# Windowed attention feeding a gated FFN on one core: FFN weights loaded as bf16 by casting DMAs from GpSimd's queue, with the loads metered

## The chip, the cores and the metric

The kernel runs on one core of a Trainium2 chip. The core has five engines, each with its own instruction stream: TensorE (PE; the profile shows its weight loads apart, as PEld), VectorE (DVE), ScalarE (ACT), GpSimd (POOL) and SyncE (SP, which only starts DMAs here). Sixteen DMA engines, shared by all queues, move data between HBM and the on-chip SBUF. Matmul results go to PSUM, eight banks of 512 fp32 columns per partition. The metric is the device time of one execution in microseconds.

## The reference

Sizes: 4 batches, 8 heads, 768 positions, head width 64; 4 sink positions and a window of 128; the FFN has 512 inputs, 2048 hidden units and 512 outputs. Inputs and output are float32.

```
scores = q @ k^T / sqrt(64)                       # per batch and head
keep   = (key < 4) | (0 <= query - key < 128)
a      = softmax(where(keep, scores, -1e9))
x      = (a @ v) with heads side by side          # 3072 tokens x 512
h      = x @ w_in                                 # 512 -> 2048
g      = h / (1 + exp(-beta * h))                 # beta: one per hidden unit
out    = g @ w_out                                # 2048 -> 512
```

## The kernel before

**Tiling.** The 3072 tokens are eight half batches of 384. A half batch has four head pairs, so there are 32 pairs in all, u = 0 to 31. Each pair runs through these steps. T: six transposes on TensorE bring q and k to head-major form, one copy takes both out of PSUM. SC: scores only for the key blocks that the window reaches. SS: scores against the sinks. ScalarE takes exp into bf16 tiles E and ES, and GpSimd masks E in place with affine selects (in even half batches VectorE multiplies the sink blocks with a mask). AV: E times v, with a column of ones that gives the softmax sum; VectorE takes the reciprocal and normalises. OT: three transposes and a copy into xT, the FFN's input in bf16.

**FFN.** An H unit is one block of 128 hidden units for one half batch: four matmuls of 384 columns, tanh on ScalarE, and one VectorE instruction that gives (tanh(beta h / 2) + 1) h, which is twice the gated value. An O quad is four matmuls of 512 columns; four quads make an output tile of 128 tokens, which one copy takes from PSUM to an output buffer `osb`, and SyncE stores. There are 128 H units and 96 O quads. The factor 1/2 that g lacks sits in w_out.

**Loads.** q, k and v come as float32 into two staging slots (`stg`), are cast to bf16 (x16, vaug) and used from there. The first half batch is loaded per head (24 DMAs of 96 KB, runs of 256 bytes per row; q and v on SyncE's queue, k on ScalarE's), the others per block of 128 tokens (nine DMAs of 256 KB per half batch, on SyncE's queue, 1024 runs of 256 bytes each). The weights are eight pieces of 1 MiB, 512 runs of 2 KB each: 0 to 3 are w_in by columns (piece j feeds H units 4j to 4j+3), 4 to 7 are w_out by rows (piece 4+j feeds the j-th quad of every O tile). Each piece lands in one of two staging buffers `wst` (L362) and two instructions of ScalarE or VectorE cast it into place (`cast_w`, L365; w_out times 0.5).

**The order.** A planner writes all instruction streams in one pass. It keeps a modelled clock per engine and for the DMA queue, and again and again takes the first step of the list OT, AV, SC, SS, T, then O or H, that its model says is ready; loads and casts are placed by `background()` before each choice. Each operation becomes a place in its engine's stream; engines run their streams strictly in order, and semaphores guard every dependency. So a modelled duration changes no work, only the order. Before the change `LOADS` puts the weight pieces 0 to 3 behind the first half batch, and 4 to 7 behind the second, all on SyncE's queue; a load is placed as soon as its buffer is free in the model.

Of the kernel before, what the change touches and what calls it, by code (L numbers as in the profile page):

```python
# [26 lines left out]
class Graph:  # L27
# [17 lines left out]
    def add(self, eng, fn, ns=0, r=(), w=(), x=(), dma=None):  # L45
# [182 lines left out]
def _program(nc, G, sb, ps, q, k, v, w_in, w_out, beta, out):  # L228
    NU = 2 * NPAIR
    NSTG, NX, NV, NT, NE, NON, NG, NTT, NOS, NWS, NKS = 2, 2, 3, 8, 3, 3, 3, 3, 3, 2, 4  # L230
    NK = NB // 2
# [9 lines left out]
    wst = sb("wst", (128, 4, 512), F32, NWS)  # L241
# [114 lines left out]
    def load_w(j):  # L356
        z = j % NWS
        if j < 4:
            src = w_in_src[:, :, j * 512:(j + 1) * 512]
        else:  # L360
            src = w_out_src[:, 4 * (j - 4):4 * (j - 3), :]
        add("sp", lambda e: e.dma_start(wst[z][:, :, :], src), 1048576 / 380, w=[("wst", z)], dma=f"dw{z}")  # L362

    def cast_w(j):
        z = j % NWS  # L365
        for h in range(2):
            src = wst[z][:, 2 * h:2 * h + 2, :]
            if j < 4:
                dst, sc = w_in16[:, 2 * h:2 * h + 2, j * 512:(j + 1) * 512], 1.0
            else:  # L370
                dst, sc = w_out16[:, 4 * (j - 4) + 2 * h:4 * (j - 4) + 2 * h + 2, :], 0.5
            eng = quickest({"act": act_ns(1024), "dve": dve_ns(1024, 1.9)})
            add(eng, copy_fn(eng, dst, src, sc), act_ns(1024) if eng == "act" else dve_ns(1024, 1.9),
                r=[("wst", z)], w=[("w16", j, h)])
# [208 lines left out]
    def HQ(T_, m):  # L583
# [5 lines left out]
        for c in range(4):  # L589
# [3 lines left out]
                r=[("w16", m // 4, c // 2), ("xT", c, T_)], x=[("B", bs[0])])  # L593
# [9 lines left out]
    def OQ(T_, t, j):  # L603
# [3 lines left out]
        for m in range(4 * j, 4 * j + 4):  # L607
# [3 lines left out]
                r=[("w16", 4 + m // 4, m // 2 % 2), ("g", T_, m)], x=[("B", bk)])  # L611
        if j == 3:
# [4 lines left out]
            add(eng, copy_fn(eng, osb[z][:, :], P[:, bk, :]), opts[eng], w=[("osb", z)], x=[("B", bk)])  # L617
# [16 lines left out]
    n_cast, n_w = [0], [0]  # L634

    def head(s):
# [25 lines left out]
        elif s == "H":  # L662
# [5 lines left out]
            t = G.at([("xT", c, T_) for c in range(4)] + [("w16", m // 4, 0), ("w16", m // 4, 1)])  # L668
            tb = banks_at(1)
            fn = lambda: HQ(T_, m)  # L670
        else:
# [3 lines left out]
            t = G.at([("g", T_, m) for m in range(4 * j, 4 * j + 4)] + [("w16", 4 + j, 0), ("w16", 4 + j, 1)])  # L675
# [11 lines left out]
    def background():  # L687
# [3 lines left out]
        while moved:  # L691
            moved = False
            i = done["load"]
            if i < len(LOADS):
                x = LOADS[i]
                at_hb = CASTS[n_cast[0]][0] if n_cast[0] < len(CASTS) else NSB
                if isinstance(x, int):
                    if x < NWS + n_w[0]:
                        load_w(x)
# [105 lines left out]
```

## Time and profile before

| | |
|---|---|
| median of 3 runs | 261.52 us (260.94 to 264.68) |
| profiled execution | 262.38 us |
| its span, first to last instruction | 260.7 us |
| granted TensorE clock, mean | 0.991 |
| TensorE busy | 228.8 us (88%) |
| ScalarE, VectorE, GpSimd busy | 166.5, 129.0, 96.7 us |
| read from HBM, written | 27.27 MB, 6.29 MB |
| first FFN matmul | 30.76 us |

In the profile's strips each character is a slice of 6.5 us, and a digit is the busy share in tenths. In its rows the bracket at the end gives the idle time before an instruction and what ended it; SPq, ACTq and POOLq are the engines' DMA issues. The bulk of the reads is over at about 120 us; the rest of the execution is FFN work on TensorE.

### The profile page before, as it was taken

How to read it: one execution, taken by the hardware profiler on the slowest of the kernel's cores; microseconds unless marked ns; L12 is line 12 of the kernel's file. 1: busy time of each engine (PE TensorE's matmuls, PEld its weight loads, DVE VectorE, ACT ScalarE, POOL GpSimd, SP SyncE). 2: the span in 40 equal slices, each digit the busy share in tenths (PEclk: the TensorE clock that was granted, in tenths of full speed). 3: DMA queues.
4: the chain of work that ended last, by engine and by line, in shares of the span. 5: the costliest groups of instructions: out<-in, count | busy, mean ns of one | idle time of the engine just before them, and what ended most of it. 6: DMA issues, size and time to landing. Idle time of an engine off the chain costs nothing.

```text
span 260.7 us, 5023 instructions
## 1 busy us (share of the span) xinstructions
PE 228.8 (88%) x1861; PEld 132.3 (51%) x1889; DVE 129.0 (49%) x285; ACT 166.5 (64%) x302; POOL 96.7 (37%) x197
## 2 busy tenths in 40 slices
PE   1307899669999999999999999999999999999995
PEld 0204456334556566655665655555555555555542
DVE  1116678553466686556666434633533453353320
ACT  2239689663898988888889874754545554565420
POOL 5205443665597897869791720000000000000000
PEclk9999999799999999999999999999999999999999
DMA  6984879799999999996101011011011111111112
GB/s 153 215 313 158 243 181 288 267 284 247 221 264 216 268 219 226 256 229 166 40 4 40 3 40 43 0 40 54 30 40 44 40 40 40 43 40 40 43 40 80
DMA packets 82856, 33.89 MB, mean 130 GB/s; under 512 B 75648, under 2 KB 75664, under 8 KB 82832
## 3 DMA queue, kind: packets, MB, share of 16 engines
q1 hardware_dynamic: 79632, 32.78, 46.3%
q10 hardware_dynamic: 3200, 0.79, 1.3%
q8 instruction: 15, 0.25, 0.4%
q14 instruction: 9, 0.07, 0.1%
HBM read 27.27 MB, written 6.29 MB: 129 GB/s over the span
## 4 chain that ended last, share of the span: by engine, by line
PE 68%; DMA 10%; ACT 9%; DVE 7%; SPq 2%; issue 2%; POOL 1%; DVEq 0%
PE P L590 30%; PE P L608 28%; DMA wst<-in_moe_w_out_dram 6%; ACT E L490 4%; DMA k_stage<-in_k_dram 3%; PE P L480 3%; DVE onorm L558 2%; SPq L353 2%; PE P L429 2%; PE P L570 2%; PE P L552 2%; DVE g L596 2%; ACT t L594 2%; DMA v_stage<-in_v_dram 1%; DVE qkT L307 1%
## 5 line engine op out<-in xcount | busy, mean ns | idle before, releaser
L596 DVE SCALAR_TENSOR_TENSOR g<-t,P 128x384 bf16<-128x384 f32 x128 | 70.5, 554 | 83.2 <-ACT t L594 68.8
L594 ACT ACTIVATE t<-P,hbeta 128x384 f32<-128x384 f32 x128 | 74.1, 583 | 50.3 <-PE P L590 47.3
L590 PE MATMUL P<-xT,w_in 128*128 128x384 bf16 x512 | 99.5, 330 | 0.0
L608 PE MATMUL P<-w_out,g 128*128 128x512 bf16 x356 | 93.2, 381 | 6.3 <-DVE w_out L308 2.3
L590 PEld LDWEIGHTS P<-xT,w_in 128*128 128x128 bf16 x512 | 49.6, 99 | 39.2 <-issue 2.0
L496 POOL TENSOR_SCALAR_AFFINE_SELECT E<-E 128x256 bf16<-128x256 bf16 (+1 forms) x112 | 52.8, 506 | 34.2 <-ACT E L490 33.8
L608 PEld LDWEIGHTS P<-w_out,g 128*128 128x128 bf16 x384 | 36.0, 98 | 39.6 <-DVE w_out L308 3.3
L490 ACT ACTIVATE E<-P 128x768 bf16<-128x768 f32 x64 | 45.0, 770 | 4.0 <-PE P L480 3.7
L552 PE MATMUL P<-vaug,E 128*128 128x65 bf16 x352 | 20.6, 201 | 1.2 <-POOL E L496 0.4
L309 ACT ACTIVATE osb<-P 128x512 f32<-128x512 f32 x22 | 13.2, 599 | 12.9 <-PE P L608 12.8
L552 PEld LDWEIGHTS P<-vaug,E 128*128 128x128 bf16 x352 | 17.8, 102 | 5.0 <-POOL E L496 1.4
L558 DVE TENSOR_TENSOR onorm<-P,rden 128x384 bf16<-128x384 f32 x32 | 17.8, 557 | 1.1
L480 PE MATMUL P<-qkT 64*128 64x128 bf16 (+1 forms) x256 | 16.8, 254 | 0.8 <-ACT E L490 0.8
L409 POOL TENSOR_SCALAR_AFFINE_SELECT vaug<-v_stage 128x512 bf16<-128x512 f32 x21 | 14.3, 681 | 3.7 <-DMA v_stage<-in_v_dram 3.7
L309 ACT ACTIVATE xT<-P 128x384 bf16<-128x384 bf16 x25 | 12.3, 505 | 5.3 <-PE P L570 5.1
L517 ACT ACTIVATE ES<-P 128x128 bf16<-128x128 f32 (+1 forms) x32 | 11.7, 398 | 6.0 <-PE P L514 5.8
L570 PE MATMUL P<-ident,onorm 128*128 128x128 bf16 x96 | 11.3, 230 | 3.8 <-DVE onorm L558 3.1
L429 PE MATMUL P<-ident,k_0 128*128 128x128 bf16 x48 | 6.0, 241 | 8.7 <-DVE k_0 L307 8.7
L480 PEld LDWEIGHTS P<-qkT 64*128 64x128 bf16 x256 | 9.1, 99 | 8.7 <-issue 3.2
L542 PE MATMUL P<-vS,ES 128*128 128x130 bf16 x64 | 13.4, 229 | 0.0
L429 PE MATMUL P<-ident,q_0 128*128 128x128 bf16 x48 | 6.0, 241 | 7.1 <-DVE q_0 L307 5.3
L570 PEld LDWEIGHTS P<-ident,onorm 128*128 128x128 bf16 x96 | 6.7, 100 | 9.7 <-DVE onorm L558 5.2
(47 smaller groups left out, 140.1 us busy)
## 6 DMA issues: line engine op xcount, KB each, us to landing
out_dram<-osb SPq DMA_DIRECT2D x24, 256.0 KB, 2.0
q_stage<-in_q_dram SPq DMA_DIRECT2D x21, 256.0 KB, 4.4
k_stage<-in_k_dram SPq DMA_DIRECT2D x21, 256.0 KB, 4.5
v_stage<-in_v_dram SPq DMA_DIRECT2D x21, 256.0 KB, 4.3
wst<-in_moe_w_in_dram SPq DMA_DIRECT2D x4, 1024.0 KB, 7.7
wst<-in_moe_w_out_dram SPq DMA_DIRECT2D x4, 1024.0 KB, 7.0
k_stage<-in_k_dram ACTq DMA_DIRECT2D x8, 96.0 KB, 2.9
q_stage<-in_q_dram SPq DMA_DIRECT2D x8, 96.0 KB, 2.8
```

The source lines that it names most:

```text
L309: return lambda e: e.activation(dst, src, AF.Copy, bias=0.0, scale=scale)
L429: add("pe", lambda e, i=i, n=n, c=c: nc.tensor.transpose(mp[:, i * HALF + c * 128:i * HALF + (c + 1) * 128], x16[n][hb % NX][:, c, 2 * hp: ...
L480: add("pe", lambda e, dst=dst, kt=kt, kc=kc, rows=rows, q0=q0, nq=nq: e.matmul(dst, kt[rows, 1, kc:kc + 128], qkT[u % NT][rows, 0, q0:q0 + ...
L490: add("act", lambda e, src=src, dst_=dst_: e.activation(dst_, src, AF.Exp, bias=0.0, scale=SCALE), act_ns(256 * n), w=[(k_, z, j) for k_ i ...
L496: add("gp", lambda e, d=d, sg=sg, at_=at_: e.affine_select(d, d, [[0, 2 * len(at_)], [sg, 128]], ALU.is_ge, 0.0, base=min(sg, 0), channel_ ...
L552: e.matmul(A[:, c0:c0 + D + 1], E[z][:, i, hh, :], vaug[vz][:, kb % NK, 2 * hp + hh, :], start=a, stop=o, skip_group_check=True), 39,
L558: add("dve", lambda e: e.tensor_tensor(onorm[on][:, :, :, :].rearrange("p m h d -> p (m h) d"), av[:, :, 0:D], rden[on][:, :].unsqueeze(2) ...
L570: add("pe", lambda e, m=m: nc.tensor.transpose(mp[:, m * 128:(m + 1) * 128], onorm[on][:, m, :, :].rearrange("p h d -> p (h d)"), ident[:, ...
L590: add("pe", lambda e, c=c: e.matmul(hp, w_in16[:, c, m * 128:(m + 1) * 128], xT[:, c, t0:t0 + HALF], start=(c == 0), stop=(c == 3)), mm_ns ...
L594: add("act", lambda e: e.activation(tt[ti][:, :], hp, AF.Tanh, bias=0.0, scale=hbeta[:, m:m + 1]), act_ns(HALF) + 93, r=["hbeta"], w=[("t" ...
L596: add("dve", lambda e: e.scalar_tensor_tensor(gt[T_ % NG][:, m, :], tt[ti][:, :], 1.0, hp, ALU.add, ALU.mult), dve_ns(HALF), r=[("t", ti)] ...
L608: add("pe", lambda e, m=m: e.matmul(P[:, bk, :], gt[T_ % NG][:, m, t * 128:(t + 1) * 128], w_out16[:, m, :], start=(m == 0), stop=(m == NM ...
```

## The change

The weights are no longer staged. `load_w` issues one DMA per piece from GpSimd's queue, with a float32 source and a bf16 destination, straight into `w_in16` or `w_out16`; the DMA rounds on its way. `cast_w` and the `wst` buffers are gone, H and O wait for the piece's DMA itself, each piece has a semaphore of its own, and the factor 1/2 moves from w_out to the copy of the output tile. The output buffers become four instead of three.

The planner's rules change with it. It costs a DMA issue 1150 ns on GpSimd and 550 on the other queues (before, 600 on SyncE and 1000 on the others). The first half batch's twelve loads are all placed at the start, before anything else. After that a load is placed only when the modelled DMA backlog is at most 3 us (`BACKLOG`), and a cast of q, k or v only when its data is due within 300 ns (`AHEAD`), where it was 500 and, in the first half batch, at once. When nothing is ready the model's clock moves on by 200 ns.

```diff
-            self.free[eng] = at + (600 if eng == "sp" else 1000)
+            self.free[eng] = at + (1150 if eng == "gp" else 550)
...
-    NSTG, NX, NV, NT, NE, NON, NG, NTT, NOS, NWS, NKS = 2, 2, 3, 8, 3, 3, 3, 3, 3, 2, 4
+    NSTG, NX, NV, NT, NE, NON, NG, NTT, NOS, NKS = 2, 2, 3, 8, 3, 3, 3, 3, 4, 4
...
     def load_w(j):
-        z = j % NWS
         if j < 4:
-            src = w_in_src[:, :, j * 512:(j + 1) * 512]
+            dst, src = w_in16[:, :, j * 512:(j + 1) * 512], w_in_src[:, :, j * 512:(j + 1) * 512]
         else:
-            src = w_out_src[:, 4 * (j - 4):4 * (j - 3), :]
-        add("sp", lambda e: e.dma_start(wst[z][:, :, :], src), 1048576 / 380, w=[("wst", z)], dma=f"dw{z}")
-
-    def cast_w(j):
...
+            dst, src = w_out16[:, 4 * (j - 4):4 * (j - 3), :], w_out_src[:, 4 * (j - 4):4 * (j - 3), :]
+        add("gp", lambda e: e.dma_start(dst, src), 1048576 / 380,
+            w=[("w16", j)], dma=f"dw{j}")
...
-            add(eng, copy_fn(eng, osb[z][:, :], P[:, bk, :]), opts[eng], w=[("osb", z)], x=[("B", bk)])
+            add(eng, copy_fn(eng, osb[z][:, :], P[:, bk, :], 0.5), opts[eng], w=[("osb", z)], x=[("B", bk)])
...
+    BACKLOG, AHEAD = 3000, 300
...
-            if i < len(LOADS):
+            if i < len(LOADS) and G.dma_free <= now + BACKLOG:
...
-                if t is not None and ok and (t <= now + 500 or hb == 0):
+                if t is not None and ok and t <= now + AHEAD:
...
+    for x in xl(0):
+        load(*x)
+        for c in range(NK):
+            mark(("in",) + x, ("stg", x[1], 0, c, x[3]))
+    done["load"] = 12
...
         if best[0] > now + 200:
...
+            G.free["pe"] = now + 200
+            continue
```

SyncE's stream behind the first half batch's loads, before: the four w_in pieces, then the second half batch (`128x8x64`), then w_out.

```order
L353 DMA v_stage<-in_v_dram 128x3x64 x2
L362 DMA wst<-in_moe_w_in_dram 128x4x512 x4
L353 DMA q_stage<-in_q_dram 128x8x64
...
L353 DMA v_stage<-in_v_dram 128x8x64
L362 DMA wst<-in_moe_w_out_dram 128x4x512 x4
L353 DMA q_stage<-in_q_dram 128x8x64
```

SyncE's stream now, from the seventh load of the second half batch on; the first output store stands between the fourth and the fifth load of the third.

```order
L352 DMA q_stage<-in_q_dram 128x8x64
L352 DMA k_stage<-in_k_dram 128x8x64
L352 DMA v_stage<-in_v_dram 128x8x64
L352 DMA q_stage<-in_q_dram 128x8x64
L352 DMA k_stage<-in_k_dram 128x8x64
L352 DMA v_stage<-in_v_dram 128x8x64
L352 DMA q_stage<-in_q_dram 128x8x64
L607 DMA out_dram<-osb 128x512
L352 DMA k_stage<-in_k_dram 128x8x64
```

No weight is left on SyncE's queue, the second half batch follows the first directly, and stores now stand among the early loads.

GpSimd's stream from the masks of the first four head pairs on (`E<-E`), before:

```order
L409 AFFINE_SELECT q_0<-q_stage 128x3x128 x3
L496 AFFINE_SELECT E<-E 128x256 x12
L409 AFFINE_SELECT q_1<-q_stage 128x512
L409 AFFINE_SELECT k_1<-k_stage 128x512
L409 AFFINE_SELECT vaug<-v_stage 128x8x64
```

and now, from the second pair's masks to the last weight piece, whose issue stands behind the masks of pair 4:

```order
L484 AFFINE_SELECT E<-E 128x256 x3
L361 DMA w_in<-in_moe_w_in_dram 128x4x512
...
L397 AFFINE_SELECT q_1<-q_stage 128x512
L397 AFFINE_SELECT k_1<-k_stage 128x512
L361 DMA w_out<-in_moe_w_out_dram 128x4x512
...
L397 AFFINE_SELECT vaug<-v_stage 128x8x64
L361 DMA w_out<-in_moe_w_out_dram 128x4x512
L484 AFFINE_SELECT E<-E 128x256
L484 AFFINE_SELECT E<-E 128x512 x2
L484 AFFINE_SELECT E<-E 128x256
L361 DMA w_out<-in_moe_w_out_dram 128x4x512
```

One w_in issue follows the masks of each of the first four pairs; three of the w_out issues stand among the casts of the second half batch's loads, and the fourth follows the next pair's masks.

TensorE's stream from the first use of the last w_out piece to the third half batch's transposes (`ident,q_0`), before:

```order
L608 MATMUL P<-w_out,g 128x512 x4
L542 MATMUL P<-vS,ES 128x130
L552 MATMUL P<-vaug,E 128x65 x4
...
L608 MATMUL P<-w_out,g 128x512 x4
L570 MATMUL P<-ident,onorm 128x128 x3
L608 MATMUL P<-w_out,g 128x512 x4
L590 MATMUL P<-xT,w_in 128x384 x4
...
L429 MATMUL P<-ident,q_0 128x128 x3
```

and now:

```order
L596 MATMUL P<-w_out,g 128x512 x4
L558 MATMUL P<-ident,onorm 128x128 x3
L530 MATMUL P<-vS,ES 128x130
L540 MATMUL P<-vaug,E 128x65 x4
...
L596 MATMUL P<-w_out,g 128x512 x12
L558 MATMUL P<-ident,onorm 128x128 x3
L596 MATMUL P<-w_out,g 128x512 x4
L578 MATMUL P<-xT,w_in 128x384 x4
L596 MATMUL P<-w_out,g 128x512 x4
L578 MATMUL P<-xT,w_in 128x384 x4
L417 MATMUL P<-ident,q_0 128x128 x3
```

Counted over the whole stream, 19 H units and 9 O quads stood ahead of those transposes before, and 18 and 11 now; more quads lie behind the wait for the last w_out piece.

More of the change, by code (lines that the diff above doesn't have):

```diff
@@ L751, in _program @@
                 break
-            pend = [G.at([("wstu", n_w[0])]) if n_w[0] < 8 else None]
-            if n_cast[0] < len(CASTS):
-                pend.append(G.at([("in",) + CASTS[n_cast[0]]]))
-            pend = [p for p in pend if p is not None and p > now]
-            assert pend, (done, n_cast, n_w)
-            G.free["pe"] = min(pend)
+            G.free["pe"] = now + 200
+            assert now < 1e6, (done, n_cast)
             continue
@@ L760, in _program @@
         if best[0] > now + 200:
[L761 to L767 removed]
+            G.free["pe"] = now + 200
+            continue
         fn()
```

43 lines of the change are left out of this document (8 added, 35 removed).

## The prediction

> **What bounds the kernel now.** I read the page first: busy time, then the strips of 40 slices (6.5 us each).
>
> ```profile
> span 260.7 us, 5023 instructions
> PE 228.8 (88%) x1861; PEld 132.3 (51%) x1889; DVE 129.0 (49%) x285; ACT 166.5 (64%) x302; POOL 96.7 (37%) x197
> PE   1307899669999999999999999999999999999995
> DMA  6984879799999999996101011011011111111112
> ```
>
> TensorE is the limit from about 60 us on; its idle time of 31.9 us (260.7 - 228.8) lies ahead of that, and there the DMA strip is at 7 to 9 while TensorE's falls to 0 and to 6. The stretches, cut at places in TensorE's program (the first FFN matmul at 31, the end of the first 16 H units at 43.1, the end of the last weight wait at 59, the third half batch's transposes at 67.09, the last matmuls at 250.2), say how much:
>
> ```profile
> core 0: us, PE busy (x) PEld busy (x) DVE busy (x) ACT busy (x) POOL busy (x), PEclk, DMA share, GB/s
> 0.00:31.00 31.00, 12.66 (x118) 7.72 (x119) 11.06 (x29) 15.06 (x29) 11.36 (x34) 1.00 0.74 213
> 31.00:43.10 12.10, 12.10 (x68) 6.89 (x67) 8.61 (x16) 9.38 (x17) 5.15 (x9) 1.00 0.91 211
> 43.10:59.00 15.90, 10.72 (x125) 6.21 (x124) 9.53 (x18) 11.51 (x18) 9.30 (x18) 0.89 0.86 289
> 59.00:67.09 8.09, 7.96 (x53) 4.15 (x55) 2.83 (x7) 3.15 (x6) 4.86 (x8) 1.00 1.04 236
> 67.09:250.20 183.11, 178.10 (x1471) 104.19 (x1494) 96.26 (x214) 126.25 (x232) 66.07 (x131) 1.00 0.37 95
> ```
>
> 18.3 us are idle before 31, 5.2 between 43.1 and 59, 0.1 up to 67.09, and 5.0 in the following 183. The chain of waits, in order of time, names what TensorE waits for early on:
>
> ```profile
> 10.29 8.03 DMA k_stage<-in_k_dram
> ...
> 30.97 8.85 PE P L590 x44
> ...
> 40.55 8.72 DMA wst<-in_moe_w_out_dram
> ...
> 50.62 7.25 DMA wst<-in_moe_w_out_dram
> ...
> 57.88 1.07 ACT w_out L309
> ```
>
> So the last head pair's k takes 8.03 us because it shares the engines with two pieces of w_in, and the last piece of w_out sets 59.0. SyncE's timeline shows why the engines aren't full all along: the four w_in issues stretch over 16.86 us, since pieces 2 and 3 wait for a staging buffer, and nothing behind them starts.
>
> ```profile
> 8.70 1.05 SPq L353 DMA_DIRECT2D v_stage<-in_v_dram  x2
> 9.79 16.86 SPq L362 DMA_DIRECT2D wst<-in_moe_w_in_dram  x4
> ```
>
> **The price of a transfer**, from three stretches: k and w_in together; the gap while SyncE waits; q, k, v alone.
>
> ```profile
> 13.00:16.60 3.60, 0.00 (x0) 0.00 (x0) 0.00 (x0) 2.10 (x7) 0.00 (x0) 1.00 1.02 348
> 20.00:26.70 6.70, 5.41 (x64) 3.39 (x64) 4.25 (x11) 6.37 (x12) 4.21 (x9) 1.00 0.47 159
> 34.00:39.60 5.60, 5.60 (x35) 3.35 (x34) 4.28 (x9) 5.26 (x10) 3.12 (x5) 1.00 1.01 229
> ```
>
> A half batch of q, k, v is 2.36 MB in runs of 256 B: 10.3 us at 229 GB/s. A weight piece is 1.05 MB in runs of 2 KB: 3.0 us at 348. The gap leaves 0.53 x 6.7 = 3.6 us of the engines unused.
>
> **What is removed.** The weight casts leave:
>
> ```profile
> L309 ACT ACTIVATE w_in<-wst 128x1024 bf16<-128x1024 f32 x4 | 4.4, 1095 | 0.7 <-DMA wst<-in_moe_w_in_dram 0.7
> L309 ACT ACTIVATE w_out<-wst 128x1024 bf16<-128x1024 f32 x2 | 2.1, 1058 | 2.0 <-DMA wst<-in_moe_w_out_dram 2.0
> L307 DVE CAST w_in<-wst 128x1024 bf16<-128x1024 f32 x4 | 3.2, 793 | 0.0
> L308 DVE TENSOR_SCALAR w_out<-wst 128x1024 bf16<-128x1024 f32 x6 | 4.7, 808 | 2.9 <-DMA wst<-in_moe_w_out_dram 2.9
> ```
>
> 6.5 us on ScalarE and 7.9 on VectorE, of which only the 1.07 us that begin at 57.88 end the chain; neither engine is the limit later (64% and 49% busy). The staging buffers go, and with them the waits in front of SyncE's loads: the second half batch's nine loads follow the first's at 9.8 instead of 26.7 us.
>
> **What is moved.** Eight weight issues go to GpSimd's queue. There each stands behind masks or load casts, and masks stand behind it; a masked E tile is what TensorE's AV matmuls wait for. No trace row shows an issue on GpSimd. The nearest are SyncE's: a weight issue without a wait took 0.37 us, a load of 1024 runs up to 1.40. I take 1.1, a middle nearer the upper row as GpSimd is the slower engine for all it does here. All eight k issues now stand first on ScalarE, 8 x 0.48 us from 0.81 on, so its table load ends near 6.1, about when TensorE's first transposes do; it is covered. The output copies take 0.5 as a factor in the same 24 instructions, and a fourth output buffer joins three whose stores land in 2.0 us while an O tile takes 4 x 0.86 us: nothing for both.
>
> ```profile
> L353 ACTq DMA_DIRECT2D k_stage<-in_k_dram x8: 420/480/507, 0.8 to 10.3; - x8
> L309 ACT ACT_TABLE_LOAD x1 | 1.3, 1283 | 3.7 <-DMA k_stage<-in_k_dram 3.7
> out_dram<-osb SPq DMA_DIRECT2D x24, 256.0 KB, 2.0
> 51.58 1.40 SPq L353 DMA_DIRECT2D k_stage<-in_k_dram  x1
> L362 SPq DMA_DIRECT2D wst<-in_moe_w_out_dram x4: 368/410/798, 39.6 to 50.6; - x4
> 12.63 0.53 ACT L309 ACTIVATE vaug<-v_stage 128x384 bf16<-128x384 f32 x1 [2.27 <-DMA v_stage<-in_v_dram]
> 22.49 4.34 POOL L496 TENSOR_SCALAR_AFFINE_SELECT E<-E 128x256 bf16<-128x256 bf16 x9 [10.90 <-ACT E L490]
> ```
>
> **The front.** The times in this part are estimates; they are to show that nothing there comes later than the transfers that the next part counts. Without w_in beside them, the first half batch's loads are served by about 11.5 (the last v's cast waited until 12.63, and its issue is as early as before). The last k no longer lands at 18.3 but with the rest. Scores of pair 0 start at about 7, its masks (0.48 each, from the x9 row) end near 10, where the first w_in piece is issued. Pairs 1 to 3 follow at the pace of ScalarE's work per pair (two exps, one small exp, two casts: some 2.9 us), so that the last pair's scores stand at 17, its masks at 20 and the first H matmul, after AV, normalisation, transposes and a copy (2.6 us), at about 22.6: 8 us earlier than 30.97. The w_in pieces are issued near 10, 14, 17 and 20 and, one after another, are in place by 28, each before its four H units start. The 16 units take 12.1 as before, to 34.9; the second half batch's k is cast by 36.
>
> **The gate.** The time of the last w_out piece follows from what the engines have carried before: 11.5, and 10.3 for the second half batch, and eight pieces. A casting transfer reads as much and writes half. No row shows one. Its price lies between 1.5 us (the write side decides) and 4.6 (it runs at the 229 GB/s of the small runs); I take 3.2, near the 3.0 row, as the 2 KB read is the same. Sum: 11.5 + 10.3 + 8 x 3.2 = 47.4. Beside it, packets of the third half batch slip in: k above got 192 KB through while two pieces went, which is a 256 B run per 2 KB run; four w_out pieces thus let 0.52 MB by, 2.3 us. With 1.3 to land (an output store lands in 2.0, of which its 256 KB are 0.8 to 1.1): **51.0**, where it was 57.88, with a cast to 59. The instruction order allows it: the last w_out issue stands behind pair 4's masks, which by the steps above end at about 43.4.
>
> From the gate to the third half batch's transposes the new order has 8 O quads, 2 H units, 2 AV and 3 output transposes. Prices from TensorE's timeline after 59 and in the chain:
>
> ```profile
> 59.00 1.04 PE L608 MATMUL P<-w_out,g 128*128 128x512 bf16 x4 [1.32 <-ACT w_out L309]
> 59.87 0.22 PE L542 MATMUL P<-vS,ES 128*128 128x130 bf16 x1
> ...
> 60.41 1.03 PE L608 MATMUL P<-w_out,g 128*128 128x512 bf16 x4
> 61.51 0.34 PE L570 MATMUL P<-ident,onorm 128*128 128x128 bf16 x3
> 61.69 1.03 PE L608 MATMUL P<-w_out,g 128*128 128x512 bf16 x3
> 62.55 0.81 PE L590 MATMUL P<-xT,w_in 128*128 128x384 bf16 x4
> 63.20 1.03 PE L608 MATMUL P<-w_out,g 128*128 128x512 bf16 x4
> ```
>
> O 0.86, AV 0.54, transposes 0.18, H 0.65: 6.9 + 1.3 + 1.1 + 0.5 = 9.8. The transposes start at 60.8, not 67.09. By then 18 H and 11 O are done instead of 19 and 9: 1.1 us more. Gain 6.3 + 1.1 = 7.4. From there TensorE does the same work; half batches 4 to 6 must arrive 6 us earlier relative to what the same engines carry (after the gate still 5.5 half batches, 57 us), and I give back 1.0 (0 to 3) for waits at their transposes. Span 260.7 - 6.4 = 254.3; around it lie 262.38 - 260.7 = 1.7, so 256.0 against the profiled run's 262.38. The median 261.52 is 0.9 below that run: **255.1 us**.
>
> **Two rules against these rows.** The quickest weight piece took 5.0 us from issue to landing, beside other loads:
>
> ```profile
> DMA to landing us min/median/max: 5.0/7.2/10.1
> ```
>  DMA: Bandwidth & Descriptors in the Trainium skill (section Anatomy of one DMA) gives a transfer issued from GpSimd 2.0 us plus its bytes at 436 GB/s, 4.4 us for a piece; by an estimate from it each piece holds the engines 2.4 us, the transfers alone end by 44.6, the last issue behind pair 4's masks (43.4 + 1.1 + 4.4 = 48.9) decides in their place, and the end comes 2.1 us earlier, near 253.0.
>
> VectorE is busy 8.61 of 12.10 us in 31 to 43.1. SBUF — State Buffer in the Trainium skill (Who interferes with whom) says that VectorE's two-port modes lock GpSimd out, and that a DMA issued there then waits for its descriptors; this speaks against the change, and no run here shows it yet. It is the second rival.
>
> **Rivals.** (1) *The casting path is slow.* At 4.6 us a piece the gate moves by 8 x 1.4 = 11.2 to 62.2; 7.4 - 11.2 - 1 gives a time 4.8 us longer, 266.3, and slower beyond. The sign turns at 7.4 / 8 = 0.9 us more per piece, 4.1. For it: the slow row exists and nothing shows casting; against: reads and packets stay those of the 348 row. Chance 0.14, half of it over 2% slower with prices past 4.6. (2) *GpSimd is held up.* If every issue costs 2.5 us (the 1.40 row, and 1.1 in which VectorE holds it up), masks and H slip by 1.4 for each of three issues ahead of the last pair's masks, 4.2, and the gate with them: gain 2.2, 259.3. For it: masks are on the chain already; against: VectorE loses the weight casts, its longest instructions with both ends in SBUF. Chance 0.15. (3) *A store blocks loads.* SyncE's new order puts the first output store between the fourth and fifth load of the third half batch; it waits for the first O tile, at gate + 1.5. Five loads follow, 1.31 MB, 5.7 us, landing and a cast of 0.6: ready at gate + 9.3 or later, against 9.8 when TensorE asks. Little cover: with 3 us late, 258.1. Chance 0.15. (4) The forecast: 0.56, its own range 252 to 258.
>
> **Chances.** This kernel's measurement tells 2%, 5.2 us, from no change: faster is below 256.3. The forecast gives it three times in four, (2) and (3) once in six: 0.47. Slower, above 266.8: 0.10, half of (1) and 0.03 for two rivals at once. Same: 0.43. The range 251.5 to 264 leaves out most of (1) and a little below.
>
> **What would show it.** Right: no k wait of 8 us early; the first H matmul near 22.6; w_out's last piece landed near 51; third transposes near 61; DMA share above 0.9 from 10 to 50. (1) shows as weight pieces over 4 us apart in time with a full DMA strip; (2) as long DMA issues on GpSimd with masks behind; (3) as transposes waiting on q or k casts while SyncE waits for a copy of the output.

## The result, and the profile after

The changed kernel takes 253.73 us (median of 4 runs, 253.14 to 254.02), the kernel before, on the same chip, 261.23 us (4 runs, 260.85 to 264.68). The ratio is 0.968, with a 95% interval of 0.960 to 0.977: faster. The profiled run took 254.02 us, with a span of 252.3 us. The page of the changed kernel, its busy times, strips and the two queues that carry loads and weights (packets, MB written, share of the 16 engines' span):

```profile
span 252.3 us, 5040 instructions
PE 229.4 (91%) x1889; PEld 132.0 (52%) x1889; DVE 121.8 (48%) x274; ACT 160.6 (64%) x298; POOL 100.3 (40%) x204
...
PE   1588955899999999999999999999999999999994
DMA  7999999969999899985011010111011011111112
...
q1 hardware_dynamic: 75408, 24.39, 39.5%
q0 software_dynamic: 4224, 4.19, 10.3%
```

The second and third slices of TensorE were 3 and 0 and are 5 and 8. The dip later, at 43 to 59 us before, now lies at 36 to 50. The stretches of the kernel after, cut at the same places of TensorE's program as those of before (first FFN matmul, end of the first 16 H units, last wait for a weight, third half batch's transposes):

```profile
core 0: us, PE busy (x) PEld busy (x) DVE busy (x) ACT busy (x) POOL busy (x), PEclk, DMA share, GB/s
0.00:20.28 20.28, 10.16 (x117) 7.41 (x118) 9.95 (x29) 11.42 (x24) 13.79 (x39) 1.00 1.00 199
20.28:32.36 12.08, 12.08 (x68) 6.67 (x65) 7.20 (x13) 9.10 (x16) 4.21 (x8) 0.86 1.15 217
32.36:50.21 17.85, 11.12 (x106) 5.99 (x105) 4.37 (x10) 9.86 (x16) 9.91 (x19) 0.81 1.11 188
50.21:60.19 9.98, 9.96 (x79) 5.42 (x80) 3.62 (x10) 2.27 (x4) 6.01 (x11) 1.00 0.73 180
```

The first FFN matmul came 10.5 us earlier (30.76 to 20.28). The last wait for a weight ends 8.8 us earlier (59.00 to 50.21), the third half batch's transposes start 6.9 us earlier (67.09 to 60.19), and from these to the end of the span the kernels take 193.6 and 192.1 us. So of the gain of 8.4 us in the span all but 1.5 us is made ahead of these transposes. Between 32.36 and 50.21 TensorE loses even more than in the like stretch before (6.7 us idle against 5.2), and the DMA share is 1.11 instead of 0.86: the transfers now come almost without gaps, and the work waits for the last of them. (A share can exceed 1, since it adds up the times of packets, which overlap: transfers alone and back to back read 0.91 to 1.12 in the first experiment.)

GpSimd's timeline gives the issues, and the chain of waits, in order of time, what ended last:

```profile
9.95 0.91 POOL L361 DMA_DIRECT2D w_in<-in_moe_w_in_dram  x1
...
18.69 0.76 POOL L361 DMA_DIRECT2D w_in<-in_moe_w_in_dram  x1
...
38.29 0.76 POOL L361 DMA_DIRECT2D w_out<-in_moe_w_out_dram  x1
...
40.95 0.76 POOL L361 DMA_DIRECT2D w_out<-in_moe_w_out_dram  x1
```

```profile
29.72 7.90 DMA v_stage<-in_v_dram
...
40.95 9.21 DMA w_out<-in_moe_w_out_dram
```

Two things are new there. A load of v (the last of the second half batch) takes 7.90 us beside two w_out pieces; its cast stands on GpSimd ahead of the third w_out issue and holds it until 38.29. And SyncE's fourth load of the third half batch is followed by the first output store, which waits from 42.3 to 51.9.

### The profile page after: what moved, and what is told of

The parts are those of the page before. It is cut to its first block, busy times and chain, and to the rows that moved or that the text cites. A ratio compares the mean times of both kernels' runs of the same rounds, so it can differ in the third digit from the quotient of the medians.

```text
span 252.3 us, 5040 instructions
## 1 busy us (share of the span) xinstructions
PE 229.4 (91%) x1889; PEld 132.0 (52%) x1889; DVE 121.8 (48%) x274; ACT 160.6 (64%) x298; POOL 100.3 (40%) x204
## 3 DMA queue, kind: packets, MB, share of 16 engines
q0 software_dynamic: 4224, 4.19, 10.3%
## 4 chain that ended last, share of the span: by engine, by line
PE 66%; SPq 11%; ACT 9%; DMA 7%; DVE 4%; issue 1%; POOL 1%; DVEq 0%
PE P L596 29%; PE P L578 26%; SPq L352 11%; ACT E L478 4%; DMA w_out<-in_moe_w_out_dram 4%; DMA v_stage<-in_v_dram 3%; PE P L540 2%; ACT t L582 2%; PE P L417 2%; PE P L558 2%; PE P L468 2%; DVE g L584 2%; DVE onorm L546 1%; ACT osb L308 1%; PE P L530 1%
## 5 line engine op out<-in xcount | busy, mean ns | idle before, releaser
L596 PE MATMUL P<-w_out,g 128*128 128x512 bf16 x384 | 98.7, 383 | 6.5 <-DMA w_out<-in_moe_w_out_dram 5.6
L578 PE MATMUL P<-xT,w_in 128*128 128x384 bf16 x512 | 98.4, 330 | 0.4 <-ACT osb L308 0.4
L484 POOL TENSOR_SCALAR_AFFINE_SELECT E<-E 128x256 bf16<-128x256 bf16 (+1 forms) x112 | 52.0, 499 | 24.6 <-ACT E L478 24.4
L540 PE MATMUL P<-vaug,E 128*128 128x65 bf16 x352 | 19.8, 199 | 0.0
L308 ACT ACTIVATE xT<-P 128x384 bf16<-128x384 bf16 x23 | 11.4, 500 | 4.5 <-PE P L558 4.4
L544 DVE RECIPROCAL rden<-P 128x6 f32<-128x6 f32 x32 | 6.1, 191 | 14.0 <-PE P L540 13.7
L306 DVE COPY qkT<-P 128x768 bf16<-128x768 bf16 x20 | 10.8, 553 | 1.7 <-PE P L417 1.5
```

The costliest lines, as they stand in the source:

```text
L308: return lambda e: e.activation(dst, src, AF.Copy, bias=0.0, scale=scale)
L484: add("gp", lambda e, d=d, sg=sg, at_=at_: e.affine_select(d, d, [[0, 2 * len(at_)], [sg, 128]], ALU.is_ge, 0.0, base=min(sg, 0), channel_ ...
L540: e.matmul(A[:, c0:c0 + D + 1], E[z][:, i, hh, :], vaug[vz][:, kb % NK, 2 * hp + hh, :], start=a, stop=o, skip_group_check=True), 39,
L578: add("pe", lambda e, c=c: e.matmul(hp, w_in16[:, c, m * 128:(m + 1) * 128], xT[:, c, t0:t0 + HALF], start=(c == 0), stop=(c == 3)), mm_ns ...
L596: add("pe", lambda e, m=m: e.matmul(P[:, bk, :], gt[T_ % NG][:, m, t * 128:(t + 1) * 128], w_out16[:, m, :], start=(m == 0), stop=(m == NM ...
```

## Experiments

The first four were run beside each other on one chip (there the kernel before took 263.48 us), the next four on a second (262.44), three more on a third (263.68), the last on the second (262.95). Compared are ratios to the kernel before, and places in the profiles.

**What a casting transfer costs.** A kernel of transfers alone; it computes nothing and stores zeros. Six stretches stand one behind the other: eight casting weight pieces from GpSimd; eight plain ones from GpSimd; eight plain ones from SyncE; eighteen loads of 256 KB in 256 B runs; the same loads with four casting pieces beside them; eight casting pieces beside VectorE copies with both ends in SBUF.

```diff
+    for j in range(8):
+        add("gp", lambda e, j=j: e.dma_start(w16[j][:, :, :], piece(j)), 0, w=[("a", j)], dma=f"a{j}")
...
+        add("gp", lambda e, j=j: e.dma_start(w32[j][:, :, :], piece(j)), 0, r=one, w=[("b", j)], dma=f"b{j}")
```

> No part of the computation is done; the output is zeros. Six stretches, each after the one before: eight casting weight pieces from GpSimd alone; eight uncast pieces from GpSimd alone; eight uncast pieces from SyncE alone; eighteen loads in runs of 256 bytes alone; eighteen more with four casting pieces beside them; eight casting pieces beside VectorE copies with both ends in SBUF. My theory (a casting piece holds the engines as an uncast one does, about 3.2 us; two queues share run by run): stretches 1 to 3 differ by under 15% and take 25 to 28 us each; stretch 5 takes the sum of its parts, 4 x 3.2 + 20 = 33 us, and its pieces are in place after some 15 us. The rival of a slow casting path: stretch 1 takes 37 us or more, stretch 2 about 25. The rival that VectorE holds up GpSimd's issues: issues in stretch 6 of 1.5 us or more and a stretch 3 us or more longer than stretch 1; mine: issues as in stretch 1, 0.8 us, and under 1 us longer.

The six stretches, by windows of its trace (length first; VectorE, GpSimd, clock, DMA share, GB/s written):

```profile
1.24:25.07 23.83, 1.07 (x2) 6.07 (x8) 1.00 1.08 176
25.07:49.63 24.56, 0.00 (x0) 5.96 (x8) 1.00 0.91 342
49.63:73.74 24.11, 0.00 (x0) 0.00 (x0) 1.00 0.95 348
73.74:97.48 23.74, 0.00 (x0) 0.00 (x0) 1.00 1.12 199
97.48:132.74 35.26, 0.00 (x0) 2.98 (x4) 1.00 1.05 193
132.74:156.72 23.98, 23.98 (x38) 6.30 (x8) 1.00 1.08 175
```

Eight pieces take 23.8 us casting, 24.6 and 24.1 plain: 3.0 us each with the last landing in it, whichever queue and whether cast or not. The casting rows show half the GB/s because only written bytes are counted. In the changed kernel the casting queue holds 10.3% of the engines' 252.3 us, 26.0 us or 3.25 per piece; the prediction had taken 3.2. Eighteen loads and four pieces together take 35.3 us, about the sum of both apart (23.7 and 11.9). In the last stretch VectorE is busy throughout, the issues take 0.79 us instead of 0.76 (6.30 and 6.07 for eight), and the stretch is 0.15 us longer than the first.

**Do the transfers set the gate?** Each weight transfer moves half of its piece, and the matmuls use that half for both; all orders stay.

```diff
-            dst, src = w_in16[:, :, j * 512:(j + 1) * 512], w_in_src[:, :, j * 512:(j + 1) * 512]
+            dst, src = w_in16[:, 0:2, j * 512:(j + 1) * 512], w_in_src[:, 0:2, j * 512:(j + 1) * 512]
...
-                hp, w_in16[:, c, m * 128:(m + 1) * 128], xT[:, c, t0:t0 + HALF],
+                hp, w_in16[:, c % 2, m * 128:(m + 1) * 128], xT[:, c, t0:t0 + HALF],
```

> The changed kernel with only half of each weight piece loaded (the matmuls read the loaded half twice, so the output is not the reference's); every stream keeps its order. If the transfers ahead of the last w_out piece set the gate, eight pieces at 1.6 us less bring it from 50.2 to about 40, TensorE's own work then decides, the third transposes start near 50 instead of 60.2 and the time is 243 to 246 us. If the order on GpSimd (masks and casts ahead of the issues) sets it, the gate moves by under 2 us and the time is 252 to 254.

244.11 us, ratio 0.927 (0.921 to 0.932), transposes at 50.34 instead of 60.19. They do: 4.2 MB less to read brought the transposes 9.85 us. TensorE's first use of the last w_out piece and these transposes, with no wait for a weight left:

```profile
40.39 0.81 PE L596 MATMUL P<-w_out,g 128*128 128x512 bf16 x3
...
50.34 0.33 PE L417 MATMUL P<-ident,q 128*128 128x128 bf16 x3
```

**The casting transfers alone.** The rules of the order are those of before; the weights go through GpSimd's queue and are cast on the way.

```diff
 (before)
-                    if x < NWS + n_w[0]:
-                        load_w(x)
-                        mark(("wstu", x), ("wst", x % NWS))
+                    load_w(x)
```

> The kernel before with casting pieces from GpSimd's queue and nothing else of the change: loads not metered, the planner's old rules. All eight issues then stand ahead of the first masks. By my theory the casting buys nothing by itself: the pieces, sharing run by run, take the engines ahead of the second half batch, whose k lands near 49 instead of 34; first FFN matmul near 27, third transposes near 67, time 258 to 263 us. If the gain comes from casting and from the freed waits on SyncE alone: 252 to 255.

262.06 us, ratio 0.998 (0.995 to 1.002): no gain. All eight pieces are issued in one row from 11.08 us on, and the second half batch's loads starve beside them; the chain has

```profile
31.80 13.09 DMA k_stage<-in_k_dram
```

and TensorE stands 6.31 us until 44.71 for the cast of that half batch's first transposes.

**The order alone.** The new rules, the weights staged and cast as before (and with the three output buffers of before).

```diff
 (after)
+                    if x < NWS + n_w[0]:
+                        load_w(x)
+                        mark(("wstu", x), ("wst", x % NWS))
...
+                if t is not None and t <= now + AHEAD:
+                    cast_w(i)
+                    n_w[0] += 1
```

> The other part alone: the planner's new rules (first half batch placed at once, loads metered, k issues first on ScalarE), with the weights staged on SyncE's queue and cast by ScalarE and VectorE as before. The last k no longer waits behind w_in, but the w_in pieces still wait for staging buffers and hold up the second half batch. Expected: first FFN matmul near 25, last w_out piece cast near 56, third transposes near 65, time 257 to 260 us: about a third of the gain. If metering is the whole gain: 253 to 255; if it is none: 261.

255.32 us, ratio 0.970 (0.964 to 0.975). This was a miss: a third of the gain was expected, nearly all of it came. It upset the theory held until then, that the gain comes from the weights no longer waiting for staging buffers. What in the order does it, the next four runs ask, the changed kernel among them.

> The changed kernel once more, beside three others on one chip, so that they can be compared with each other. Its profile had its last w_out wait at 50.21, the third half batch's transposes at 60.19 and a span of 252.3 us. Both theories expect the ratio to the kernel before that was measured, 0.968 (0.960 to 0.977). What is asked is its distance from the next run: if the casting transfers are worth what the two profiles differ by (transposes at 60.19 against 62.40), this kernel is 2.2 us the faster, 0.8 to 0.9%; if the difference was the chip or chance, less than 1 us lies between them.

> The new order rules with the weights staged on SyncE and cast on ScalarE and VectorE as before, once more. Theory 1 (the casting transfers add 2 us to what the order gives): 2.2 us slower than the changed kernel on the same chip, 1.7 to 2.7. Theory 2 (the order is the whole change): within 1 us of it.

The changed kernel: 253.75 us, ratio 0.966 (0.962 to 0.971). The order alone: 255.69 us, 0.973 (0.968 to 0.978). Between them lie 1.9 us, as the first theory had it, though the two intervals overlap a little. That is what the casting transfers are worth in this order, together with the fourth output buffer, which was not tried by itself.

**Two edits of the order.** The kernel before, in which only the twelve loads of the first half batch are placed ahead of all else, so that ScalarE issues its eight k loads first, and the first half batch's casts are placed when due.

```diff
 (before)
-                if t is not None and ok and (t <= now + 500 or hb == 0):
+                if t is not None and ok and t <= now + 500:
...
     consts()
+    for x in xl(0):
+        load(*x)
+        for c in range(NK):
+            mark(("in",) + x, ("stg", x[1], 0, c, x[3]))
+    done["load"] = 12
```

> The kernel before with two edits alone: the twelve loads of the first half batch are placed before anything else, so that ScalarE's eight k issues no longer stand behind its table load and casts, and its casts are placed when they are due and not at once. The loads on SyncE, the staging and the casts of the weights are those of before; no load is metered. Theory 1 (the late k of the first half batch is what the new order mends): no k load of 8 us, the first H matmul near 22 (before 30.97; 21.9 with all the new order rules), the third half batch's transposes near 62.5, time 254.5 to 257.5 on a chip where before takes 262. Theory 2 (the metering and the later placing of casts bring the gain at the gate): first H near 22, but the gate stays near 57 to 59 because the weights still wait for their staging buffers, transposes at 65 to 67, time 259.5 to 262.

255.62 us, ratio 0.973 (0.968 to 0.978): the same as all the new rules without the casting transfers. Of its profile: ScalarE's k issues (duration, first and last start; the last stood at 10.3 before), SyncE's four w_in issues, and TensorE's first H matmul, last wait for w_out and third transposes.

```profile
L353 ACTq DMA_DIRECT2D k_stage<-in_k_dram x8: 472/510/511, 0.8 to 4.5; - x8
```

```profile
10.02 9.93 SPq L362 DMA_DIRECT2D wst<-in_moe_w_in_dram  x4
```

```profile
20.71 12.24 PE L590 MATMUL P<-xT,w_in 128*128 128x384 bf16 x64
...
51.54 1.04 PE L608 MATMUL P<-w_out,g 128*128 128x512 bf16 x4 [0.90 <-DVE w_out L308]
...
59.50 0.33 PE L429 MATMUL P<-ident,q 128*128 128x128 bf16 x3
```

With staging buffers and weight casts in place, the first H matmul comes at 20.71, the gate at 51.54 and the transposes at 59.50. The waits for staging buffers are still there (9.93 us for four issues), but they were 16.86 in the kernel before. The chain of the kernel before shows why, once one reads on behind the k load of 8.03 us:

```profile
18.34 0.06 DVE k_0 L307
...
20.33 0.45 ACT ES L517 x2
20.78 0.94 ACT w_in L309
```

Two casts free a staging buffer. One stood on ScalarE behind an exp that needed the last k, the other on VectorE behind the cast of that k (it began at 20.89). So the late k held the w_in pieces, these held SyncE, and with it the second half batch and w_out. The two edits were not tried apart: that the early k does it, and not the later placing of the casts, rests on this chain.

**Without the metering.** The changed kernel with the backlog bound out of reach.

```diff
-    BACKLOG, AHEAD = 3000, 300
+    BACKLOG, AHEAD = 10**9, 300
```

> The changed kernel without the metering (the backlog bound is set out of reach, nothing else): all eight casting issues stand on GpSimd ahead of its first mask. Theory 1 (the engines serve the queues run by run, so 2 KB runs push the 256 B runs of q, k and v aside): the first half batch's k is in by about 26 and its q and v by about 34, the first H matmul comes near 37 instead of 20.28, TensorE's 33 us of work from there to the third half batch's transposes put these at about 70, time 261 to 265, no faster than before. Theory 2 (only the sum of the bytes sets the gate, and the metering adds nothing): transposes near 60, time 252 to 256.

263.17 us, ratio 1.005 (1.001 to 1.009): all the gain is gone. The eight pieces are issued before the first mask, and in the chain and on TensorE stand

```profile
13.44 17.66 DMA v_stage<-in_v_dram
```

```profile
37.23 10.70 PE L578 MATMUL P<-xT,w_in 128*128 128x384 bf16 x64
```

The first H matmul was expected near 37, the time at 261 to 265. A load of 96 KB in 256 B runs takes 17.66 us beside 2 KB runs. Between 12 and 32 us the casting queue moved 3163 packets and SyncE's queue 3162: while both had work, as many packets of the one were served as of the other, and a packet of the weights (2 KB read, 1 KB written) carries several times what a run of 256 B does. The order in which bytes arrive counts here, not their sum alone: the last weight piece had landed by 36.9 (issued at 9.8, 27.1 us to land), and nothing could use any of them before 37.23.

**The GpSimd rival.** A fill of a scratch tile, 0.98 us, behind each weight issue.

```diff
+        add("gp", lambda e: e.memset(scr[:, :], 0.0), 0, r=["scr"] if j else [], w=["scr"])
```

> The changed kernel with a fill of a scratch tile, about 1 us, on GpSimd behind each of the eight weight issues, so that an issue costs GpSimd some 1.8 us instead of 0.76 to 0.91. Theory 1 (the second rival: masks and H matmuls slip with the three issues ahead of the last pair's masks, and the gate with them): first H matmul near 23.3, the gate and the transposes 3 us later, time 256.5 to 258. Theory 2 (the gate is set by what the transfers have carried, and GpSimd's delays lie beside them): first H matmul up to 3 us later, but the gate moves less than 1 us, time 253.5 to 255.

256.97 us, ratio 0.971 (0.966 to 0.977). The first H matmul moves by 2.8 us to 23.04, the last w_out wait by 1.6 to 51.76, the transposes by 1.4 to 61.60. Between the two theories: of the 2.8 us by which the H units slip about half reach the gate. The time cannot be told from that of the changed kernel (0.966, 0.962 to 0.971); the places in the profile can.

**The store rival.** The first three output stores are issued from ScalarE's queue.

```diff
-            add("sp", lambda e: e.dma_start(out_t[3 * T_ + t], osb[z][:, :]), 262144 / 300, r=[("osb", z)],
+            o = add("sp", lambda e: e.dma_start(out_t[3 * T_ + t], osb[z][:, :]), 262144 / 300, r=[("osb", z)],
                 dma=f"do{z}")
+            if os_i[0] <= 3:
+                o.eng = "act"
```

> The changed kernel with its first three output stores issued from ScalarE's queue, so that SyncE's loads no longer stand still behind the first store (42.3 to 51.9). Theory 1 (TensorE waits for w_out there, not for these loads; the five freed loads only share the engines with the last w_out piece): gate 50.2 to 51.5, transposes 60 to 61.5, time 253 to 255. Theory 2 (the third rival: the store holds the loads back at a price): transposes and what follows earlier, time 250 to 252.5.

254.77 us, ratio 0.966 (0.960 to 0.973), that of the changed kernel. SyncE's fifth load of the third half batch went out at 41.59 instead of 52.32. In the profiled run, the slowest of the four with 257.31 us, the last w_out wait moved from 50.21 to 51.81 and the transposes to 63.02 (the clock fell behind that wait, and an O quad at 53.50 took 1.90 us), but not by these loads. In its chain of waits stand

```profile
29.35 9.77 DMA v_stage<-in_v_dram
...
42.44 9.09 DMA w_out<-in_moe_w_out_dram
```

The ninth load of the second half batch, over before the freed loads began, took 9.77 us instead of 7.90, and so the last piece was issued 1.5 us later; it landed as fast as before (9.09 us, 9.21 there). The store that stands in front of the loads costs nothing that can be measured.

**Holding the loads on purpose.** The first load of the third half batch waits until the third w_out piece (piece 6 of 0 to 7) has landed.

```diff
+            if (hb, n, c) == (2, "q", 0):
+                o.deps += [(p, True) for p in G.writers[("w16", 6)].values()]
```

> The changed kernel with one wait more: the first load of the third half batch on SyncE waits until the third piece of w_out (piece 6 of 0 to 7) has landed. All instructions and their orders are those of the changed kernel. There, four loads of the third half batch run beside the w_out pieces (issued 30.62 to 42.3), and the ninth load of the second half batch, for which the third w_out issue waits on GpSimd, took 7.9 us. Theory 1 (these four loads take the engines from w_out run by run): that ninth load lands by about 35, the last piece is issued near 38 and lands at 44 to 46 instead of 50.2, the third half batch's nine loads start near 42 and take 10.3 us, so the transposes come at 55 to 57 instead of 60.19, time 249.5 to 251.5. Theory 2 (the engines carry the same sum in any order, and what the weights win the third half batch loses): w_out lands earlier, but TensorE waits for the third half batch's casts, transposes at 59 to 61, time 253 to 255.

252.46 us, ratio 0.955 (0.950 to 0.960), below the changed kernel's interval. The mechanism is that of the first theory, but its size isn't: the last w_out wait ends at 48.33, not at 44 to 46, the transposes start at 58.09, not at 55 to 57. Its chain has

```profile
30.15 7.50 DMA v_stage<-in_v_dram
...
40.98 7.08 DMA w_out<-in_moe_w_out_dram
```

The last piece landed in 7.08 us instead of 9.21. But the ninth load of the second half batch still took 7.50 us: what made it slow was the two w_out pieces beside it, not the four loads that were taken away, and so the last two pieces were issued at 38.33 and 40.98 as before. The last run moved these two issues ahead of that load's cast.

```diff
+    late = [o for o in G.ops if o.dma in ("dw6", "dw7")]
+    for o in late:
+        G.ops.remove(o)
+    i = G.ops.index(ninth[0])
+    G.ops[i:i] = late
```

> The kernel of the run hold6 with one thing moved: the issues of the last two w_out pieces stand on GpSimd ahead of the cast of the second half batch's ninth load instead of behind it and behind masks (there they were issued at 38.33 and 40.98, and the DMA share fell to 0.8 to 1.0 at 30 to 36 and at 38 to 42, against 1.22 when full). All else is as in hold6. Theory 1 (weights that come late still set the gate): the pieces are issued near 35, the last wait for w_out ends near 46.5 instead of 48.33, the third half batch's loads start near 43 and its transposes come at 56 to 57.5 instead of 58.09, time 0.5 to 1.5 us less than hold6, ratio to before 0.949 to 0.953. Theory 2 (in hold6 the third half batch's loads decide already, the second pair's transposes there followed their k cast): the gate moves by 1.5 us and the time by less than 0.5 us, ratio 0.953 to 0.957. Theory 3 (four pieces queued at once starve the ninth load, and TensorE waits for that): AV of the second half batch later, time 253 to 255 and ratio 0.960 to 0.968.

250.70 us, ratio 0.954 (0.949 to 0.959): not to be told from 0.955. That is the time of the second theory, but its reason fails: the gate was to move by 1.5 us. The pieces are issued from 32.97 on. GpSimd's and TensorE's timelines of this kernel:

```profile
32.97 1.51 POOL L363 DMA_DIRECT2D w_out<-in_moe_w_out_dram  x2
...
57.03 0.61 POOL L399 TENSOR_SCALAR_AFFINE_SELECT k<-k_stage 128x512 bf16<-128x512 f32 x1 [0.29 <-DMA k_stage<-in_k_dram]
```

```profile
40.91 1.89 PE L598 MATMUL P<-w_out,g 128*128 128x512 bf16 x4 [1.39 <-DMA w_out<-in_moe_w_out_dram]
...
45.08 1.82 PE L598 MATMUL P<-w_out,g 128*128 128x512 bf16 x4
...
48.03 0.81 PE L598 MATMUL P<-w_out,g 128*128 128x512 bf16 x3
...
57.98 0.33 PE L419 MATMUL P<-ident,q 128*128 128x128 bf16 x3
```

TensorE no longer waits for the last two pieces (no wait is noted at 45.08 and 48.03), yet it reaches the last one only 0.3 us earlier than in the run before, because its work ahead of that runs at half the speed, an O quad in 1.8 us instead of 1.04; the windows show why in the section on the hardware. The last k cast ahead of the transposes ends at 57.64, 0.3 us before they start, so that the third half batch's loads have next to no slack left.

## Why the prediction was right, and where it wasn't

The forecast, 255.1 us with a range of 251.5 to 264, and faster as the likeliest, held. Its steps:

- **The front.** First w_in issues near 10, 14, 17 and 20: measured 9.95, 13.43, 16.02 and 18.69. First H matmul 22.6: measured 20.28. The reason given, that the last k lands with the rest when w_in isn't beside it, fits the kernel with the two edits, whose first H matmul comes at 20.71. The 16 units were to take 12.1 us: measured 12.08, part of it at half the clock (0.86 in the mean).
- **What is removed.** This step read the profile wrongly in good part. It took the four w_in issues over 16.86 us, with SyncE waiting for a staging buffer, as a cost of the staging, and let the buffers' removal give the second half batch its early start. The kernel with the two edits alone keeps the buffers and gets 6.8 of the 8.7 us (262.44 to 255.62, against 253.75); the kernel with the removal alone gets none (0.998). Of the 16.86 us some 7 went with the late k, seen from SyncE; the other 9.93 stayed with the buffers. Without buffers the second half batch's loads do go out early, but beside w_in, and little comes of it: the nine start from 10.39 to 29.72 in the changed kernel, from 20.00 to 31.60 in the one with the two edits. The step counted as two causes, the k load and the staging buffer, what was mostly one, and did not follow the chain from the one to the other, though both stood in it.
- **The gate.** 11.5 + 10.3 + 8 x 3.2 plus what slips in, 51.0: measured 50.21. The price of a casting piece, the widest of the unknown costs, was 3.25 in the kernel and 3.0 alone. That the sum came so near is in part luck, for errors in its terms cancel. All four loads that SyncE had issued slipped in by 50.2, 1.05 MB and not 0.52, which is 4.6 us at the 229 GB/s and not 2.3; nine loads by themselves took 11.9 us with their landing (23.74 for eighteen), and not 10.3; but eight pieces took 23.8 us with theirs, and not 25.6 and 1.3. That the sum says nothing of the order is its weak point: without metering the engines carry the same sum, and the transposes come at 68.11.
- **From the gate to the transposes.** 9.8 and 60.8: measured 9.98 and 60.19.
- **What is given back.** This term of the sum was mis-sized. From the transposes to the end 1.1 us less was expected for the order of H and O, and 1.0 us more (0 to 3) for loads that come late: measured 193.6 - 192.1 = 1.5 us less, so 0.4 beyond the 1.1 instead of 1.0 back. These 1.4 us and the 0.6 at the transposes are the 2.0 us by which the span of 254.3 was too long. The loads moved along with the work: SyncE issued the last one at 117.31 before and 112.30 after. In the last run above, whose transposes start another 2.2 us earlier, the rest takes 192.1 us again (250.1 - 58.0). Only the run before that one gives back 1.0 us (251.2 - 58.1 = 193.1), and there the transposes wait for a k cast (0.54 us).
- **Rivals.** The casting path is not slow (3.0 us a piece, against the 4.1 at which its sign turned). GpSimd pays 0.76 to 0.91 us an issue, below the 1.1 taken, and even 1 us more on each moves the gate by 1.6 only. The store in front of the loads costs nothing that can be measured. That the order could be lost to the weights themselves, as in the kernel without metering, was no rival, and should have been: it takes the whole gain (ratio 1.005), and in this kernel only the bound of 3000 in the planner stands against it.

Of the two rules weighed, the one of DMA: Bandwidth & Descriptors in the Trainium skill (section Anatomy of one DMA) gives 4.4 us for a piece, from which the prediction's estimate made 253.0 us; the time came out near that, but not in its way: the last piece was issued at 40.95, not at 44.5, and took 9.21 us to land. SBUF — State Buffer in the Trainium skill (Who interferes with whom) lets VectorE's two-port modes hold up a DMA issued from GpSimd; little of that shows here: in the last stretch of the transfers, with VectorE busy throughout, eight issues took 6.30 us instead of 6.07, and the stretch 23.98 instead of 23.83. In which mode these copies ran the trace does not say.

What stays open: the 1.9 us that the casting transfers add are seen as a difference of two kernels, but what makes them (the weight casts, the waits for staging buffers, the fourth output buffer) was not tried apart. In one pair of profiles the last w_out waits end 2.4 us apart (52.45 and 50.02) and the transposes start 1.4 us apart (61.14 and 59.77), in the other pair 3.5 (53.71 and 50.21) and 2.2 (62.40 and 60.19). The kernel with the two edits has its transposes as early as the changed one, at 59.50, and then takes 193.8 us to the end instead of 192.0; 0.4 of that is work not yet done there (20 H units and 9 O quads instead of 18 and 11, at 0.65 and 0.86), the rest was not traced.

## What to carry to other kernels

Where the queues share the DMA engines run by run, look first at when the loads in small runs are issued: one that comes behind pieces in large runs takes several times as long (a load of 96 KB 17.66 us here, against a median of 3.6 for v in the changed kernel), and an engine's wait for a buffer further on can be that same load, passed on through the instructions queued behind it. A sum of the bytes gives the earliest time of a gate, but only an order in which each queue holds back what isn't needed yet gets there; here the waits for a staging buffer had done part of that, and when they go, a bound on the backlog or a wait for the piece before has to take their place. Taking conversions off engines that aren't the limit is worth little (at most 1.9 of 8.7 us here).

## What the runs showed of the hardware

The clock that TensorE is granted falls to half behind a stall, and stays there for a time while TensorE is busy again. The prediction had left it out. Windows of the changed kernel, TensorE's busy time in the second column, the clock third from the end:

```profile
36.00:38.00 2.00, 0.21 (x2) 0.00 (x0) 0.00 (x0) 2.00 (x5) 0.32 (x1) 1.00 1.24 222
38.00:40.00 2.00, 0.59 (x3) 0.32 (x4) 0.00 (x0) 0.58 (x2) 1.99 (x4) 1.00 1.22 196
40.00:42.00 2.00, 0.87 (x10) 0.27 (x8) 0.00 (x0) 1.26 (x2) 1.99 (x5) 0.73 1.24 246
42.00:44.00 2.00, 1.82 (x6) 0.71 (x7) 0.00 (x0) 0.26 (x1) 1.66 (x4) 0.50 1.27 230
44.00:46.00 2.00, 2.00 (x25) 1.34 (x23) 0.75 (x2) 0.59 (x2) 0.00 (x0) 0.50 1.22 198
46.00:48.00 2.00, 1.72 (x11) 0.67 (x7) 0.36 (x1) 1.36 (x2) 1.27 (x3) 0.56 1.21 205
```

TensorE had waited for the first w_out piece:

```profile
39.41 1.02 PE L596 MATMUL P<-w_out,g 128*128 128x512 bf16 x4 [3.20 <-DMA w_out<-in_moe_w_out_dram]
...
42.18 1.89 PE L596 MATMUL P<-w_out,g 128*128 128x512 bf16 x4 [1.32 <-DMA w_out<-in_moe_w_out_dram]
```

The clock is at 0.50 from about 40.9 to 47.8 (the means of 0.73 in 40 to 42 and 0.56 in 46 to 48 give these ends), and an O quad takes 1.89 us instead of 1.04. TensorE: Matmul & The Clock Gate in the Trainium skill (Part 1: The HAM clock gate) says that the clock is at half after an idle window of about 3.4 us and full again after one of sustained work; the stall of 3.20 us is near that, though the fall came 1.5 us after its end, and the return took 6.8 us, about twice that window, with TensorE waiting until 42.18 and then busy at 42 to 46 for 3.8 of 4 us. Read in windows of 0.25 us, the first 100 us of all kernels' traces have seventeen such dips, and each lasts 3.4 or 6.8 us, none any time between. The changed kernel has one of 3.4 us at its first H units too (from 20.5 to 23.9, after TensorE was busy for 0.70 of the 2 us from 18 to 20); the 16 units take 12.08 us there and 10.67 with half pieces, where no dip occurs.

In the last of the runs above the clock held the O quads back after their weights had come; the same window of that run, and of the run before it:

```profile
42.00:46.00 4.00, 4.00 (x32) 2.28 (x31) 1.11 (x3) 1.86 (x3) 0.77 (x3) 0.50 1.03 194
...
42.00:46.00 4.00, 2.66 (x33) 1.49 (x32) 1.11 (x3) 2.03 (x4) 2.93 (x7) 1.00 1.21 195
```

About as many matmuls take 4.00 us at 0.50 and 2.66 at 1.00, where the dip had come sooner (34.9 to 38.3). What a full clock throughout would have been worth was not tried, since nothing in these kernels sets it. Besides, a transfer that casts cost what a plain one costs (23.83 and 24.56 us for eight), and one on GpSimd's queue what one on SyncE's does (24.11).
